# A new place for one product, four PSUM banks instead of six, and a rule for starting half-array steps

## The chip, the cores and the metric

One core of one Trainium2 chip runs the whole kernel. The metric is device time in microseconds (us), lower is better; it is the time of one execution, and of several executions the median counts. PE is TensorE (matrix products into PSUM, which has eight banks), DVE is VectorE, ACT is ScalarE, POOL is GpSimd, and SP issues the DMAs.

## The reference

Four batches of eight heads go through sliding-window attention with a few sink positions; the result is mixed along the sequence by a rank-32 product and sent through a two-layer network with a residual.

```
scores = scale * q @ k.T               # 768 positions, head size 64, 8 heads, 4 batches
keep = (pos_k < n_sink) | (0 <= pos_q - pos_k < window)
a = softmax(where(keep, scores, -1e9))
x = (a @ v), heads side by side        # (4, 768, 512)
h = x.transpose(0, 2, 1) @ U @ V       # rank 32, along the sequence
u = x + h.transpose(0, 2, 1)
out = u + maximum(u @ w_ch1, 0) @ w_ch2   # 512 -> 2048 -> 512
```

## The kernel before

The kernel doesn't issue instructions as it walks through the work. It first collects **steps** (class `Plan`): each is a short piece of work for one engine (some may run on one of two or three engines), with the tiles that it reads and writes, and a priority. `Plan.order` then runs a list scheduler, `forward`, several times, keeps the best order, and the steps are issued in it, so that each engine's instructions stand in a fixed order. In `forward`, whenever an engine is free, the steps that are ready stand in `can`, sorted by priority, and the first is picked. PSUM banks are a ring of eight (`self.bank`): a step that opens a bank (`takes`) is ready only when a bank is free, and a bank is given back when the last step on it is done.

The steps on PE are of two kinds. **Half-array steps** (`tiled=True`) use 64 of the array's 128 rows or columns, two products side by side: the attention scores (line L665, one step is a query block of a head pair, two products into two banks) and the attention values (L750). All others use the whole array. The planner adds `SWITCH` to a step's duration when it changes from one kind to the other, and once a half-array step has run, it prefers further half-array steps that are ready. It has no rule for when a run of them may begin.

The order of the large pieces is: attention of batch 0; the network of batch 0 (`ffn`, L958 to L960 and L980) with the attention of batch 1 between; then the networks of batches 1, 2 and 3 (`ffn_joint`, nearly all of it L1118), with the attention of batches 2 and 3 between the products of batch 1's network. At the end of each attention the last blocks are transposed (L715), the sink columns are transposed (L827, "sink transposes" below) and mixed in (L840), and the columns are transposed and mixed (L857, L880, L881, L921). While batch 1's network runs, weight sums for later rounds are made (`prepare`, tiles `spare`) and sent to DRAM (`ws<-spare`) by DVE, POOL and ACT.

`ffn_joint` computes both layers on 2x2 blocks with seven block products instead of eight. It runs in two rounds for a batch, six in all. In each round, the first layer `l1` makes for four pairs of hidden blocks the four blocks `h[0]` to `h[3]` (named `x11`, `x12`, `x21`, `x22` after); then `second` adds seven products into three pairs of banks, called `A`, `E` and `C`. One call of `second` runs over the four pairs and writes both banks of its pair: 4 x 2 x 3 matmuls of 128x384. `A` goes on accumulating over four calls, `E` over two, and `C` has one. After each call `gather` has DVE add both banks to result tiles (L1123), and a later call on the same bank may start only when that read is done. The calls before, in the order in which they are written:

```
A(x11) E(x12-x11) A(x22-x11) C(x21) A(x22-x12) E(x22) A(x21-x11)
```

As the bank pair `C` is opened while `A` and `E` are both in use, six banks are held at that point, and two are left for the attention steps and for the next round's first layer.

Of the kernel before, what the change touches and what calls it, by code (L numbers as in the profile page):

```python
# [42 lines left out]
ROUNDS = 14  # L43
SLACK = 0.0344
SWITCH = 0.2
BACKLOG = 3.0
SAME = 0.11
PRICE = {"DVE": 3.0, "ACT": 1.5, "POOL": 1.5}
# [218 lines left out]
class Plan:  # L267
# [91 lines left out]
    def forward(self):  # L359
# [9 lines left out]
        def at(s, e):  # L369
# [6 lines left out]
                return max(t, free[n - 1] if len(free) >= n else 1e12)  # L376
            return t

        def elsewhere(s, e, end):

            for x, (dur, _, _) in s.ways.items():
                if x != e:
                    t = max(avail[x], at(s, x))
                    queue = sum(o.ways[x][0] for o in ready[x]
                                if (o.prio, o.n) < (s.prio, s.n) and at(o, x) <= t and len(o.ways) == 1)
                    if t + queue + dur * PRICE[x] < end - 1e-9:
                        return True
            return False
# [8 lines left out]
        done = 0  # L397
        while done < len(self.steps):
            turn = sorted((max(avail[e], min(at(s, e) for s in lst)), e) for e, lst in ready.items() if lst)
            pick = None  # L400
            for t, e in turn:
                if t > 1e11:
                    break
                can = sorted((s for s in ready[e] if at(s, e) <= t + 1e-9), key=lambda s: (s.prio, s.n))
                if e == "PE" and tiled:
                    can.sort(key=lambda s: not s.tiled)
                pick = next((s for s in can if len(s.ways) == 1 or not elsewhere(s, e, t + s.ways[e][0] * PRICE[e])), None)
                if pick is not None:
                    break
            if pick is None:  # L410
                t, e = turn[0]
                pick = min((s for s in ready[e] if at(s, e) <= t + 1e-9), key=lambda s: (s.prio, s.n))
            s = pick
# [63 lines left out]
class Fast:  # L477
# [625 lines left out]
    def ffn_joint(self, b, prio):  # L1103
# [90 lines left out]
        def gather(banks, to, out=None):  # L1194
# [7 lines left out]
        wa = lambda layer, j, o: lambda i: (self.wd[layer][i], lambda: self.wd[layer][i]()[  # L1202
            :, :, CORNER[(j, o) if layer == 0 else (o, j)]])
        wc = lambda layer, k: lambda i: (self.ws[layer][i], lambda: self.ws[layer][i]()[:, :, k])
        x11, x12, x21, x22 = range(4)
        r11, r22, r12, r21 = (rest(o, c) for o, c in ((0, 0), (1, 1), (0, 1), (1, 0)))
        for start in range(0, NF // 2, ROUND):
            pairs = range(start, start + ROUND)
            last = pairs[-1] == NF // 2 - 1
            done = lambda o, c: (o, c) if last else None  # L1210
            for i in pairs:
                l1(i)
                prio += 7.3
            A, E, C = ([self.bank(), self.bank()] for _ in range(3))
            second(A, x11, wa(1, 0, 0), True)
            gather(A, r11)
            second(E, x11, wc(1, 0), True, (x12, x11))
            gather(E, r22)
            second(A, x11, wc(1, 1), False, (x22, x11))
            gather(A, r12)  # L1220
            second(C, x21, wa(1, 1, 0), True)
            gather(C, r11, done(0, 0))
            second(A, x12, wc(1, 2), False, (x22, x12))
            gather(A, r22, done(1, 1))
            second(E, x22, wc(1, 3), False)
# [392 lines left out]
```

## Time and profile before

| What | us |
|---|---|
| three timed runs | 699.42, 699.63, 703.04 |
| their median | 699.63 |
| the profiled execution | 701.17 |
| span of its instructions | 699.4 |
| PE busy | 677.2 (97% of the span) |
| DVE busy | 540.2 (77%) |
| ACT busy | 441.2 (63%) |
| POOL busy | 268.9 (38%) |

The profiled execution has 1.8 us outside its span of instructions. A busy PE may still run slower than it could: a matmul of 128x384 is shown with 0.33 to 0.34 us, since matmuls are pipelined, and what tells its cost is the time from one start to the next. The granted clock of PE is a share of its full speed.

### The profile page before, as it was taken

The page shows a single profiled execution, that of the slowest core. Times are in us where ns is not written, and L with a number is a line of the kernel's source. Part 1 is how long each engine was busy: PE and PEld are TensorE (multiplying, and loading weights), DVE is VectorE, ACT ScalarE, POOL GpSimd, SP SyncE. Part 2 cuts the span into 40 slices and gives each one's busy share as a digit, 9 for nine tenths or more (in the row PEclk, how much of TensorE's full clock was granted, in tenths as well). Part 3 has the DMA queues.
Part 4 walks back from the last instruction along what each step waited for, and adds up shares of the span by engine and source line. Part 5 has one row for each costly group of instructions (what it writes and reads, how often), then busy time and mean ns, then how long its engine had stood idle before and what let it go on. Part 6 is the DMA issues. An engine that isn't in the chain of part 4 may idle for free.

```text
span 699.4 us, 12892 instructions
## 1 busy us (share of the span) xinstructions
PE 677.2 (97%) x3986; PEld 598.0 (85%) x3986; DVE 540.2 (77%) x1493; ACT 441.2 (63%) x1192; POOL 268.9 (38%) x305
## 2 busy tenths in 40 slices
PE   7988799999999999999999999999999999999996
PEld 6666678787889978878878889989999998999996
DVE  7999989999986976868886999746747975673673
ACT  5988678759585477976776786345426634543551
POOL 3565575646373433735554574300200330020020
PEclk9999999999999999999999999999999999999999
DMA  8559797999976689885789764899888899888885
GB/s 276 169 176 355 246 375 264 351 310 396 370 249 230 248 271 355 274 270 182 241 291 322 263 225 128 287 363 292 252 249 253 251 294 354 256 250 249 254 253 192
DMA packets 135118, 190.37 MB, mean 272 GB/s; under 512 B 10240, under 2 KB 106112, under 8 KB 135040
## 3 DMA queue, kind: packets, MB, share of 16 engines
q1 hardware_dynamic: 134752, 189.06, 81.4%
q8 instruction: 34, 0.56, 0.3%
q10 hardware_dynamic: 288, 0.39, 0.2%
q14 instruction: 44, 0.36, 0.2%
HBM read 140.91 MB, written 48.50 MB: 271 GB/s over the span
## 4 chain that ended last, share of the span: by engine, by line
PE 76%; DVE 15%; DMA 4%; ACT 3%; issue 1%; POOL 0%; DVEq 0%; ACTq 0%; POOLq 0%
PE bank L1118 47%; PE bank L980 8%; PE bank L665 5%; PE bank L750 3%; PE bank L958 2%; PE bank L959 2%; PE bank L960 2%; PE bank L715 2%; DVE spare L548 2%; DMA ws<-spare 2%; DMA w<-wd 2%; DVE nt L132 1%; DVE p L674 1%; DVE w L548 1%; DVE bank L672 1%
## 5 line engine op out<-in xcount | busy, mean ns | idle before, releaser
L1118 PE MATMUL bank<-w,w 128*128 128x384 f32 x1044 | 206.6, 339 | 0.2 <-DMA w<-ws 0.2
L1118 PEld LDWEIGHTS bank<-w,w 128*128 128x128 f32 x1044 | 183.0, 189 | 4.2 <-DMA w<-ws 2.1
L550 POOL TENSOR_TENSOR w<-uh,w 128x384 fp32r<-128x384 f32 x18 | 19.7, 1092 | 165.9 <-ACT w L541 161.0
L677 ACT ACTIVATE p<-p,mn 128x132 f32<-128x132 f32 x192 | 75.9, 398 | 8.8 <-DVE mn L674 8.2
L1118 PE MATMUL bank<-spare,w 128*128 128x384 f32 x336 | 76.4, 342 | 0.7 <-ACT xhl L541 0.6
L133 POOL TENSOR_TENSOR spare<-nt,big 128x512 int32<-128x512 int32 x32 | 52.3, 1639 | 42.9 <-DVE nt L132 19.4
L980 PE MATMUL bank<-w,hh 128*128 128x512 f32 x192 | 63.5, 412 | 2.8 <-ACT w L541 2.4
L1123 DVE TENSOR_TENSOR big<-bank,big 128x384 f32<-128x384 f32 x84 | 44.6, 553 | 27.8 <-PE bank L1118 27.1
L1118 PEld LDWEIGHTS bank<-spare,w 128*128 128x128 f32 x336 | 59.1, 188 | 5.8 <-issue 3.7
L550 POOL TENSOR_TENSOR spare<-spare 128x128 f32<-128x128 f32 (+1 forms) x52 | 37.9, 739 | 56.2 <-DVE spare L548 16.1
L665 PE MATMUL bank<-kp,qp 64*128 64x260 f32 (+1 forms) x360 | 53.5, 406 | 0.0
L674 DVE CUSTOM_DVE_ANT_0 p<-bank,mask 128x132 f32<-128x132 f32 x192 | 50.3, 287 | 3.1 <-PE bank L665 2.3
L672 DVE COPY_PREDICATED bank<-past,bank 128x128 f32<-128x128 int32 x160 | 41.3, 289 | 7.4 <-PE bank L665 6.9
L958 PE MATMUL bank<-ul,w 128*128 128x384 f32 x128 | 45.1, 353 | 0.0
L980 PEld LDWEIGHTS bank<-w,hh 128*128 128x128 f32 x192 | 35.2, 192 | 11.6 <-ACT w L541 2.7
L665 PEld LDWEIGHTS bank<-kp,qp 64*128 64x128 f32 x360 | 31.7, 194 | 14.9 <-issue 5.9
L541 ACT COPY nt<-bank 128x384 f32<-128x384 f32 x35 | 16.6, 475 | 44.0 <-PE bank L1118 44.0
L548 DVE TENSOR_TENSOR spare<-spare 128x128 f32<-128x128 f32 (+1 forms) x98 | 39.2, 422 | 6.1 <-DMA ws<-spare 3.7
L725 POOL TENSOR_SCALAR_AFFINE_SELECT oph<-oph 128x384 f32<-128x384 f32 x64 | 36.0, 579 | 19.6 <-ACT oph L541 19.5
L959 PE MATMUL bank<-uh,w 128*128 128x384 f32 x128 | 43.2, 337 | 0.0
L960 PE MATMUL bank<-uh,w 128*128 128x384 f32 x128 | 43.2, 337 | 0.0
L750 PE MATMUL bank<-oph,vp 128*64 128x256 f32 (+1 forms) x448 | 42.9, 341 | 0.0
(245 smaller groups left out, 1588.4 us busy)
## 6 DMA issues: line engine op xcount, KB each, us to landing
w<-ws SPq DMA_DIRECT2D x192, 256.0 KB, 3.9
w<-wd SPq DMA_DIRECT2D x144, 256.0 KB, 4.1
big<-in_w_dram SPq DMA_DIRECT2D x32, 512.0 KB, 5.9
ws<-spare SPq DMA_DIRECT2D x32, 512.0 KB, 4.9
wd<-w SPq DMA_DIRECT2D x32, 384.0 KB, 5.8
kp<-in_k_dram SPq DMA_DIRECT2D x12, 396.0 KB, 4.8
qp<-in_q_dram SPq DMA_DIRECT2D x12, 384.0 KB, 5.4
vp<-in_v_dram SPq DMA_DIRECT2D x12, 384.0 KB, 4.3
```

The costliest lines, as they stand in the source:

```text
L133: {"POOL": lambda: nc.gpsimd.tensor_tensor(out() if out else x(), words(t())[:, :n], x(), ALU.add)},
L548: ways = {"DVE": (dve(n), lambda: nc.vector.tensor_tensor(dst(), a(), b(), op), pool)}
L550: ways["POOL"] = (gps(n), lambda: nc.gpsimd.tensor_tensor(dst(), a(), b(), op), True)
L665: nc.tensor.matmul(st()[:, :wd], qr()[at, q0:q0 + P], kr()[at, k0:k0 + wd], start=True, stop=True)
L674: add("DVE", dve(SW), lambda st=st, row=row, at=at, wd=wd, qb=qb, mn=mn: nc.vector.tensor_tensor_reduce(row(), st()[:, wd - SW:wd], self.m ...
L677: add("ACT", act(SW) + 0.22, lambda row=row, at=at, mn=mn, sm=sm: nc.scalar.activation(row(), row(), AF.Exp, bias=at(mn), scale=-1.0, accu ...
L750: nc.tensor.matmul(pa()[i * D:(i + 1) * D, at:at + hi - lo], vr()[:, i, kb, :], mv, start=first, stop=last, skip_group_check=True)
L958: nc.tensor.matmul(ph()[:, :CH], wh, ul()[:, c, :], start=n == 0, stop=False)
L959: nc.tensor.matmul(ph()[:, :CH], wl, uh()[:, c, :], start=False, stop=False)
L960: nc.tensor.matmul(ph()[:, :CH], wh, uh()[:, c, :], start=False, stop=n == NC - 1)
L980: nc.tensor.matmul(acc[k](), a()[:, sl], w()[:, :, at, m:m + P].rearrange("p d o j -> p o d j"), start=not begin and i == 0 and j == 0, st ...
L1118: nc.tensor.matmul(bank()[:, :CH], w()[:, at:at + P], u()[:, d, :] if n > 1 else u(), start=first and i == 1, stop=last and i == 3 * n, sk ...
```

## The change

Two edits that do not depend on each other. In `forward`, when PE last ran a whole-array step and both kinds are ready, half-array steps are taken out of `can` unless at least `TOGETHER` = 2 of them are ready and the ring has banks for two, or one has been ready for more than `HOLD` = 3.0 us; if nothing else is ready, they stay. In `ffn_joint`, the product into `C` is written first instead of fourth, and its `gather` comes before that of `A`; the first output block is sent out after `A`'s sum instead of `C`'s. `C`'s banks are given back before `E` is opened, so four banks are held at a time, not six. The new order of the calls, in which two calls on `A` now follow each other:

```
C(x21) A(x11) E(x12-x11) A(x22-x11) A(x22-x12) E(x22) A(x21-x11)
```

```diff
@@ -43,6 +43,8 @@
 SLACK = 0.0344
 SWITCH = 0.2
+TOGETHER = 2
+HOLD = 3.0
 BACKLOG = 3.0
@@ -376,6 +378,9 @@
                 return max(t, free[n - 1] if len(free) >= n else 1e12)
             return t
 
+        def free(s, t):
+            return sum(f[0] <= t for f in s.takes[0].ring.free) if s.takes else 0
+
@@ -404,6 +409,11 @@
                 can = sorted((s for s in ready[e] if at(s, e) <= t + 1e-9), key=lambda s: (s.prio, s.n))
                 if e == "PE" and tiled:
                     can.sort(key=lambda s: not s.tiled)
+                elif e == "PE":
+                    few = [s for s in can if s.tiled]
+                    if few and len(few) < len(can) and (
+                            len(few) < TOGETHER or sum(len(s.takes) for s in few[:TOGETHER]) > free(few[0], t)):
+                        can = [s for s in can if not s.tiled or t - at(s, e) > HOLD] or can
@@ -1212,14 +1222,14 @@
             A, E, C = ([self.bank(), self.bank()] for _ in range(3))
+            second(C, x21, wa(1, 1, 0), True)
+            gather(C, r11)
             second(A, x11, wa(1, 0, 0), True)
-            gather(A, r11)
+            gather(A, r11, done(0, 0))
             second(E, x11, wc(1, 0), True, (x12, x11))
             gather(E, r22)
             second(A, x11, wc(1, 1), False, (x22, x11))
             gather(A, r12)
-            second(C, x21, wa(1, 1, 0), True)
-            gather(C, r11, done(0, 0))
             second(A, x12, wc(1, 2), False, (x22, x12))
             gather(A, r22, done(1, 1))
             second(E, x22, wc(1, 3), False)
```

The steps are the same ones in number and kind, but the whole program is ordered anew, after the first 28 rows of PE. Lines behind the edits are numbered up to 10 higher in the changed kernel (L665 is L675 there, L1118 is L1128). Counted over the whole order, PE changes into half-array steps and back 61 times before and 49 times after: 9 and 9 times in batch 0's attention, 19 and 15 in batch 0's network, 33 and 25 in batch 1's network. Runs of a single score step number 20 before and 2 after.

**First place, PE,** at the start of batch 3's attention, in batch 1's network. Before (`kp`, `qp` are keys and queries, L880 and L881 the mixing of batch 2):

```order
L1118 MATMUL bank2_163<-w4_173,w3_172 128x384 x2
L665 MATMUL bank3_164<-kp0_462,qp0_471 128x132
L665 MATMUL bank0_161<-kp0_462,qp0_471 128x132
L1118 MATMUL bank6_167<-w5_174,w3_172 128x384
L1118 MATMUL bank6_167<-w4_173,w3_172 128x384 x2
L1118 MATMUL bank2_163<-w5_174,w3_172 128x384 x3
L665 MATMUL bank4_165<-kp0_462,qp0_471 128x260
L665 MATMUL bank3_164<-kp0_462,qp0_471 128x260
L1118 MATMUL bank6_167<-w5_174,w3_172 128x384 x3
L880 MATMUL bank5_166<-xhl0_2501,ust0_681 128x512
L881 MATMUL bank5_166<-xhl1_2513,ust0_681 128x512
L665 MATMUL bank0_161<-kp0_462,qp0_471 128x260
```

The same place after:

```order
L675 MATMUL bank5_166<-kp0_468,qp0_478 128x132
L675 MATMUL bank0_161<-kp0_468,qp0_478 128x132
L675 MATMUL bank7_168<-kp0_468,qp0_478 128x260
L675 MATMUL bank1_162<-kp0_468,qp0_478 128x260
L1128 MATMUL bank2_163<-w5_174,w3_172 128x384 x3
L1128 MATMUL bank6_167<-w5_174,w3_172 128x384 x3
L890 MATMUL bank3_164<-xhl0_2604,ust0_447 128x512
L891 MATMUL bank3_164<-xhl1_2610,ust0_447 128x512
L1128 MATMUL bank2_163<-w5_174,w3_172 128x384 x3
L675 MATMUL bank5_166<-kp0_468,qp0_478 128x260
L675 MATMUL bank0_161<-kp0_468,qp0_478 128x260
L675 MATMUL bank4_165<-kp0_468,qp0_478 128x260
```

The first five score steps of the head pair stand in five runs of one before, and in a run of two and a run of three after (its last rows are not shown).

**Second place, DVE,** at the end of batch 2's attention. The reciprocal (L687, L697 after) of the last softmax sums is waited for by the last transposes on PE; the rows on `spare` belong to `prepare` and may wait for a `ws<-spare` DMA. Before:

```order
L687 RECIPROCAL r_3590<-r_3590 128x6
L674 ISA p1_2911,mn_3588<-bank0_161,mask_97 128x132
L674 ISA mn_3588 128x1
L542 CAST hh0_3047<-ul1_3507 128x384
L548 TENSOR_TENSOR spare1_176<-spare1_176 128x128
L548 TENSOR_TENSOR hh1_3051<-ul1_3507,hh0_3047 128x384
L548 TENSOR_TENSOR spare1_176<-spare1_176 128x128
L542 CAST hl0_3152<-uh0_3018 128x384
L548 TENSOR_TENSOR ul1_3507<-ul1_3507 128x384
L687 RECIPROCAL r_3645<-r_3645 128x6
```

After:

```order
L684 ISA p1_2943,mn_3603<-bank7_168,mask_97 128x132
L684 ISA mn_3603 128x1
L731 TENSOR_TENSOR oph0_3679<-bank4_165,tri_113 128x2x128
L731 TENSOR_TENSOR oph1_3685<-bank1_162,tri_113 128x2x128
L1133 TENSOR_TENSOR big0_89<-bank0_161,big0_89 128x384
L697 RECIPROCAL r_3697<-r_3697 128x6
L558 TENSOR_TENSOR spare1_176<-spare1_176 128x128
L552 CAST w5_174<-uh0_2979 128x384
```

Before, six instructions, two of them on `spare`, stand between the last score block's minimum and the reciprocal; after, three stand there, none of them on `spare`, and the row on `spare` follows the reciprocal.

**Third place, PE,** in the last round of batch 3's network, around the third call on `A`. Before (`A` is bank2 and bank5, `C` is bank6 and bank1):

```order
L1118 MATMUL bank6_167<-hh1_3051,w2_171 128x384
L1118 MATMUL bank6_167<-hh0_3047,w2_171 128x384 x2
L1118 MATMUL bank1_162<-hh1_3051,w2_171 128x384
L1118 MATMUL bank1_162<-hh0_3047,w2_171 128x384 x2
L1118 MATMUL bank6_167<-hl1_3160,w2_171 128x384
L1118 MATMUL bank6_167<-hl0_3152,w2_171 128x384 x2
L1118 MATMUL bank1_162<-hl1_3160,w2_171 128x384
L1118 MATMUL bank1_162<-hl0_3152,w2_171 128x384 x2
L1118 MATMUL bank2_163<-w4_173,w3_172 128x384 x3
L1118 MATMUL bank5_166<-w4_173,w3_172 128x384 x3
```

After (`A` is bank0 and bank5, `E` ends in bank1):

```order
L1128 MATMUL bank0_161<-hl1_3241,w2_171 128x384
L1128 MATMUL bank0_161<-hl0_3227,w2_171 128x384 x2
L1128 MATMUL bank5_166<-hh1_3149,w2_171 128x384
L1128 MATMUL bank5_166<-hh0_3130,w2_171 128x384 x2
L1128 MATMUL bank5_166<-hl1_3241,w2_171 128x384
L1128 MATMUL bank5_166<-hl0_3227,w2_171 128x384 x2
L1128 MATMUL bank1_162<-w5_174,w3_172 128x384
L1128 MATMUL bank1_162<-w4_173,w3_172 128x384 x2
L1128 MATMUL bank0_161<-w4_173,w3_172 128x384 x3
L1128 MATMUL bank5_166<-w4_173,w3_172 128x384 x3
```

Before, all 24 matmuls of `C` stand between `A`'s second and third call. After, 9 matmuls stand between bank0's last product and its next one (6 of bank5, 3 of bank1), and 6 for bank5.

## Rows read from the trace of the kernel before

**Rows 1.** The page's first section: busy time, share and instructions of each engine.
```profile
PE 677.2 (97%) x3986; PEld 598.0 (85%) x3986; DVE 540.2 (77%) x1493; ACT 441.2 (63%) x1192; POOL 268.9 (38%) x305
```

**Rows 2.** Stretches: length; PE, PEld, DVE, ACT, POOL busy; granted clock; DMA share, GB/s.
```profile
0.00:100.00 100.00, 87.28 (x494) 67.11 (x496) 88.28 (x307) 76.24 (x226) 54.64 (x68) 0.97 0.76 259
100.00:240.00 140.00, 139.93 (x802) 115.84 (x799) 126.50 (x339) 100.25 (x269) 79.53 (x80) 1.00 0.86 308
240.00:448.00 208.00, 205.64 (x1314) 175.16 (x1313) 172.45 (x552) 154.02 (x474) 106.31 (x135) 0.99 0.78 255
448.00:700.00 252.00, 244.34 (x1382) 239.87 (x1380) 153.01 (x297) 110.69 (x225) 28.46 (x23) 1.00 0.85 271
```

**Rows 3.** Timeline of PE: start us, us, instruction, count; whole-array products alone.
```profile
520.10 1.21 PE L1118 MATMUL bank<-spare,w 128*128 128x384 f32 x6
521.15 1.20 PE L1118 MATMUL bank<-w,w 128*128 128x384 f32 x6
```

**Rows 4.** Timeline of PE: a run of three score steps and a single one.
```profile
381.99 1.58 PE L665 MATMUL bank<-kp,qp 64*128 64x260 f32 x12
383.51 1.34 PE L1118 MATMUL bank<-w,w 128*128 128x384 f32 x6
384.78 0.71 PE L665 MATMUL bank<-kp,qp 64*128 64x260 f32 x4
385.42 0.44 PE L1118 MATMUL bank<-spare,w 128*128 128x384 f32 x1
```

**Rows 5.** Timeline of PE: the end of batch 2's attention; in brackets idle time and releaser.
```profile
311.75 0.49 PE L715 MATMUL bank<-ident,p 128*128 128x128 f32 x3
311.99 0.77 PE L1118 MATMUL bank<-w,w 128*128 128x384 f32 x3
313.35 0.92 PE L715 MATMUL bank<-ident,p 128*128 128x128 f32 x3 [0.60 <-ACT p L695]
314.48 0.55 PE L715 MATMUL bank<-ident,p 128*128 128x128 f32 x3 [0.20 <-POOL p L698]
314.78 0.77 PE L1118 MATMUL bank<-w,w 128*128 128x384 f32 x3
315.86 0.71 PE L827 MATMUL bank<-ident,first0q 128*128 128x128 f32 x3 [0.31 <-ACT first0q L541]
316.22 2.27 PE L1118 MATMUL bank<-w,w 128*128 128x384 f32 x6
318.29 0.84 PE L827 MATMUL bank<-ident,first0k 128*128 128x128 f32 x3
318.79 1.47 PE L1118 MATMUL bank<-hh,w 128*128 128x384 f32 x5
```

**Rows 6.** The stretch of low clock within it, columns as in Rows 2.
```profile
316.08:319.49 3.41, 3.41 (x14) 3.31 (x13) 2.50 (x5) 2.65 (x8) 1.85 (x3) 0.51 0.58 181
```

**Rows 7.** Timelines of DVE and ACT ahead of these transposes.
```profile
310.35 0.29 DVE L548 TENSOR_TENSOR spare<-spare 128x128 f32<-128x128 f32 x1 [1.46 <-DMA ws<-spare]
...
312.68 0.18 DVE L687 RECIPROCAL r<-r 128x6 f32<-128x6 f32 x1
...
312.89 0.99 ACT L695 ACTIVATE p<-p,r 128x132 f32<-128x132 f32 x3 [2.00 <-DVE r L687]
...
313.58 0.85 POOL L698 TENSOR_TENSOR p<-p,r 128x396 f32<-128x396 f32 x1
```

**Rows 8.** Timeline of PE: the end of batch 3's attention.
```profile
414.31 0.69 PE L1118 MATMUL bank<-w,w 128*128 128x384 f32 x3
415.65 0.97 PE L840 MATMUL bank<-pst,vsh 128*128 128x384 f32 x4 [0.65 <-DVE pst L548]
...
425.88 0.40 PE L880 MATMUL bank<-xhl,ust 128*128 128x512 f32 x1
426.78 0.50 PE L881 MATMUL bank<-xhl,ust 128*128 128x512 f32 x1 [0.50 <-DVE xhl L548]
```

**Rows 9.** The page's groups: the sums that read the banks after each call.
```profile
L1123 DVE TENSOR_TENSOR big<-bank,big 128x384 f32<-128x384 f32 x84 | 44.6, 553 | 27.8 <-PE bank L1118 27.1
```

## The prediction, as it was put on record

> **What bounds the kernel now.** I read the page's engine totals first [rows 1]: PE is busy 97% of the span of 699.4 us, the next engine, DVE, 77%. Then a table of stretches, to see where this holds [rows 2]. In the first 100 us, batch 0's attention and the first weights, PE is idle for 13 us while DVE is at 88%: there the chain through DVE sets the pace. From 100 us on PE is busy nearly always, in batch 0's network (100 to 240), in batch 1's (240 to 448) and in the last two (448 to 700). So a change counts in these stretches if it takes time out of PE's own stream, and busy time doesn't show that; the distance from one start to the next does. Whole-array products of 128x384 start every (521.15 - 520.10) / 6 = 0.175 us [rows 3]. What PE needs beyond that is what the change can give back or add. The timeline of PE shows two places where it does: each run of half-array steps, and the ends of the attentions, where the steps depend on each other.
>
> **The change, part by part.**
>
> *Fewer runs of half-array steps.* Four stretches follow each other [rows 4]: a run of three score steps takes 383.51 - 381.99 = 1.52 us (12 matmuls of the trace are three steps), six whole-array products 1.27, a run of one step 0.64. Two steps more cost 0.88 us, 0.44 each, so 0.64 holds 0.20 us that belong to the run. The six products took 1.27 instead of 6 x 0.175 = 1.05, so 0.22 us more are lost where they take over and give back. One run costs 0.20 + 0.22 = 0.42 us beside its steps; I take 0.40, since the 0.175 is the tightest spacing there is and mixed products have slightly more. [...]
>
> The order holds 61 runs before and 49 after, 4 fewer in batch 0's network and 8 fewer in batch 1's, both bound by PE: 12 x 0.40 = 4.8 us less. The lower bound is 8 x 0.40 = 3.2: in batch 0's network DVE is busy 126.5 of 140 us [rows 2], so 1.6 us won on PE there could be lost waiting for DVE.
>
> *Longer runs.* They need banks while they go on: each step opens two, and what frees them is a copy and a reduction on DVE. With four instead of six banks held by the second layer, two steps fit at once; a third waits for DVE. Bounds: 0 where banks are free, as in the run of three above, and 0.3 us a run for some 10 runs of three or more. I take +0.5 us.
>
> *The end of batch 2's attention.* This is the worst place after the first 100 us. From 311.99 to 318.79 PE runs 12 whole-array products and four transposes of three blocks [rows 5]. At 0.175 and at 0.24 (311.99 - 311.75) that is 2.10 + 0.96 = 3.06 us; it took 6.80, so 3.74 were lost. Half of it is idle or slow around the transposes, which wait for the scaled weights `p`. [...] What was late? ACT waited 2.00 us for the reciprocal, which DVE ran at 312.68; ahead of it on DVE stands a `spare` row that sat 1.46 us until a `ws<-spare` DMA had landed [rows 7]. The two transposes that wait for it lost 313.35 - 311.99 - 0.52 = 0.84 and 314.48 - 313.35 - 0.24 = 0.89 us, together less than these 2.00. In the new order the `spare` rows stand behind this reciprocal, so the 2.00 us go. But its cover on PE shrinks: between the last score step and the first of these transposes the order had 30 whole-array products and has 24 now, 6 x 0.175 = 1.05 us less. The first transpose, 0.84 late before, would be 0.84 - 2.00 + 1.05 = -0.11: just in time. [...] I take 3.2 of the 3.74 us as gained; bounds 0 (something else is late) and 3.74.
>
> *The other ends.* At the end of batch 3's attention PE waited twice: 415.65 - 414.31 = 1.34 us for three products (0.8 lost) because the sink mixing needs `pst`, which ACT and DVE make from the sink transposes; and 0.90 us for one product of the column mixing that needs `xhl` (0.67 lost, against 0.23 us without a wait) [rows 8]. In the new order batch 3 has 12 instead of 9 products to cover the first wait and 9 instead of 6 for the second, so most of both goes. But batches 1 and 2 now have what batch 3 had: all 24 column transposes in one piece with only 6 short products ahead of the mixing, and in batch 2 9 products between the sink transposes and their mixing. By the same rows that is 2 x 0.67 + 0.8 = 2.1 us new, about 1.1 gone: +1.0 us, bounds -1.1 and +2.1.
>
> *`A` after `A`.* A call on `A` may start when DVE has read the bank. A read takes 0.55 us [rows 9], the two banks' reads follow each other on DVE, and the rows of the third place leave 9 products (1.6 us) for the first bank and 6 (1.05) for the second. Before, 24 products (4.2 us) stood there. DVE has 39% idle after 448 us [rows 2], and with a signal each way the second read just fits if DVE is free. What is queued behind a late read on DVE is the making of the next call's operands. Six rounds have one such turn each: 0 where the cover holds, 1.0 us (both reads, uncovered) where it is gone, so 0 to 6 us. I take 0.7.
>
> *At no cost:* `C` first. Its operand `x21` is the last that the first layer makes, but only the fourth pair needs that; the three pairs before it are 18 products, 3.2 us, over a ReLU, a cast and a subtraction of about half a us each. If that cover went, it would be some 2 us a round. Its four weight DMAs a round move ahead of `A`'s on SP, none is added, and the DMA load after 448 us (0.85) stays. The first 100 us have nine runs before and after, and the work ahead of the first network is the same to within a few rows on DVE: 0, with 1.5 us either way for a new order.
>
> **The sum:** -4.8 + 0.5 - 3.2 + 1.0 + 0.7 = -5.8 us. Against the profiled span of 699.4 that is 693.6, or 695.4 for the profiled execution (701.17, 1.8 us outside the span). The median of the shown runs is 1.5 us below that execution, so I set the gain against the median: 699.63 - 5.8 = **693.8 us**. For this kernel some 0.5%, 3.5 us, is what a measurement can tell from no change.
>
> **The rivals.**
>
> *The time comes out elsewhere (no change).* The runs are fewer, but the new order has its own late chain. For it: such a stall is made by chance of order, as the `spare` row was, and sixteen of these sums with their DMAs still lie in batch 1's network. Against it: there is one such stall of over 1 us on PE in 340 us before. Price: with the 3.7 us of [rows 5] at another place and the ends at +2.1, -4.8 + 0.5 + 2.1 + 0.7 = -1.5: 698.1 us.
>
> *DVE takes back what PE wins.* Batch 0's network is at 90% on DVE, the start at 88% [rows 2]. Then the 1.6 us there are lost and the start is 1.5 us longer: 696.9 us, also within the bound.
>
> *Four banks starve PE (slower).* At each `A`-`A` turn DVE comes late, PE stops for 1.0 us, and its clock falls as in [rows 6]: half speed for 3.4 us costs 1.7. Six turns are 16 us, instead of the 0.7 above: 709 us. It decides from about 10 us lost at the turns in all (6.5 won elsewhere and 3.5 beyond), that is four of six turns with a fallen clock. Against it: after 448 us the clock is 1.00 throughout with banks read between products all the time [rows 2]. [...]
>
> **How the numbers follow.** Forecast as summed, 690.5 to 696.0: 0.62. Stall elsewhere: 0.19. DVE takes it back: 0.13. Starved: 0.06. That the change doesn't do what it says is no case, since the order holds the 49 runs. The first case is faster by more than 0.5% (below 696.1), the middle two lie within, with 0.02 of theirs beyond on the slow side, where several stalls meet. Faster 0.62, same 0.30, slower 0.08. The likeliest case alone has 690.5 to 696.0; the range goes on to 699.5, over most of the middle two cases, and leaves out about 2 in 10.
>
> **What would show it.** Half-array runs in PE's timeline: 49, each still with 0.4 us beside its steps. Granted clock 1.00 from 100 us to the end, and no wait of the last transposes of batch 2 over 0.3 us. The sink mixing or `xhl` waits now in batches 1 and 2. Waits of PE for the sums of L1133 at six places, under 0.3 us each. It would be wrong if the clock falls anywhere after 100 us, if a DVE row on `spare` waits ahead of softmax work, or if the first network begins more than 2 us later.

## The result, and the profile after

The change made the kernel slower: a median of 704.99 us (nine runs, 703.19 to 707.82) against 699.94 us for the kernel before (nine runs, 698.60 to 703.48), a ratio of 1.0068 with a 95% interval of 1.0043 to 1.0093. The profiled execution took 704.28 us, with a span of 702.6 us instead of 699.4.

The page's engine totals and one group, which answer to [rows 1, 9] (the lines of `kernel.py` are up to ten higher now):

```profile
PE 673.0 (96%) x3986; PEld 598.2 (85%) x3986; DVE 536.4 (76%) x1506; ACT 435.5 (62%) x1197; POOL 266.0 (38%) x305
...
L1133 DVE TENSOR_TENSOR big<-bank,big 128x384 f32<-128x384 f32 x84 | 44.5, 552 | 26.1 <-PE bank L1128 26.1
```

PE is busy for 4.2 us less, yet the span is 3.2 us longer, so PE stands idle more. The stretches of [rows 2], now, say where:

```profile
0.00:100.00 100.00, 85.40 (x471) 65.01 (x472) 87.69 (x298) 75.32 (x227) 49.70 (x67) 0.91 0.74 253
100.00:240.00 140.00, 137.85 (x800) 114.07 (x799) 117.82 (x339) 95.00 (x268) 69.20 (x72) 1.00 0.84 305
240.00:448.00 208.00, 206.72 (x1344) 180.02 (x1343) 181.51 (x582) 150.99 (x470) 114.37 (x137) 1.00 0.81 266
448.00:700.00 252.00, 243.07 (x1376) 239.07 (x1374) 149.36 (x290) 114.18 (x233) 32.70 (x31) 1.00 0.84 266
```

By 100 us PE has run 471 matmuls, 23 fewer than before, at a mean granted clock of 0.91 instead of 0.97. From 240 to 448 us it has run 30 more, and the clock is 1.00.

To compare kernels by stage I work out **lost time**: from each matmul's start to the next, less the spacing that its shape has in an undisturbed row (0.174 us for 128x384, 0.231 for 128x512, and so on), summed. The rest, 619 us, is the same work in all kernels. I take three stages: the *start* (to the first product of batch 1's network, 245.9 us before and 251.4 after), the *middle* (to the last product of the last attention, 445.4 and 454.3), and the *tail*. Lost time of the profiled executions, in us:

```
            start   middle  tail    sum
before      43.1    25.4    5.6     74.1
changed     47.9    19.6    9.5     77.0
difference  +4.8    -5.8    +3.9    +2.9
```

**The middle went as forecast.** This is PE's timeline at the end of batch 2's attention in the changed kernel, which answers to [rows 5]:

```profile
319.98 0.49 PE L725 MATMUL bank<-ident,p 128*128 128x128 f32 x3
320.23 1.30 PE L1128 MATMUL bank<-hl,w 128*128 128x384 f32 x6
321.36 0.49 PE L725 MATMUL bank<-ident,p 128*128 128x128 f32 x3
321.61 0.77 PE L1128 MATMUL bank<-w,w 128*128 128x384 f32 x3
322.22 0.49 PE L837 MATMUL bank<-ident,first0q 128*128 128x128 f32 x3
322.55 0.49 PE L837 MATMUL bank<-ident,first0k 128*128 128x128 f32 x3
322.79 1.83 PE L1128 MATMUL bank<-w,w 128*128 128x384 f32 x9
325.42 0.79 PE L850 MATMUL bank<-pst,vsh 128*128 128x384 f32 x3 [0.79 <-DVE pst L558]
```

No transpose waits, six products take 321.36 - 320.23 = 1.13 us, and the clock does not fall (1.00 from 240 to 448 us, as above). The new wait is for `pst`, 0.79 us, where the prediction put 0.8; PE shows none of the `xhl` waits that it put at 0.67 each at the ends of batches 1 and 2.

**The start.** The longest waits of PE in the first 100 us of the changed kernel (us in total, times, longest):

```profile
PE bank L931 <- DVE t L918: 3.6, 1, 3.6
PE bank L990 <- ACT w L551: 3.3, 1, 3.3
PE bank L990 <- DVE w L558: 1.6, 1, 1.6
```

In the kernel before, the longest waits at these two lines were 2.6, 2.4 and 0.9 us. This is PE's timeline at the second and third of them:

```profile
80.88 0.34 PE L970 MATMUL bank<-uh,w 128*128 128x384 f32 x1
84.52 0.80 PE L990 MATMUL bank<-w,hh 128*128 128x512 f32 x1 [3.30 <-ACT w L551]
86.94 0.80 PE L990 MATMUL bank<-w,hh 128*128 128x512 f32 x1 [1.62 <-DVE w L558]
```

And these are the windows of low clock in the start (columns as in [rows 2]):

```profile
15.80:22.60 6.80, 6.49 (x28) 4.38 (x29) 5.47 (x38) 4.86 (x20) 3.04 (x5) 0.50 0.43 141
63.60:67.00 3.40, 3.40 (x12) 3.40 (x12) 3.37 (x8) 3.40 (x9) 2.91 (x3) 0.50 1.00 325
84.10:90.90 6.80, 4.76 (x10) 3.43 (x11) 6.30 (x14) 2.60 (x5) 2.66 (x2) 0.50 0.75 276
```

The granted clock is 0.50 behind the first wait and from the end of the second on, and once earlier, 17.0 us in all; before it was 6.8 us, at 60 and 84 us.

Of the 4.8 us, 2.1 are lost before the first network begins (66.7 us instead of 64.6) and 2.7 in batch 0's network. There PE also waits for DVE after 100 us (100 to 251.4 us), where the kernel before shows no wait:

```profile
PE bank L990 <- DVE hl L979: 1.5, 2, 1.4
PE bank L968 <- DVE hl L979: 0.5, 1, 0.5
```

**The tail.** PE's timeline in the last round of the changed kernel, at the turn from one call on `A` to the next:

```profile
680.79 0.69 PE L1128 MATMUL bank<-hh,w 128*128 128x384 f32 x3
681.32 0.69 PE L1128 MATMUL bank<-hl,w 128*128 128x384 f32 x3
681.85 0.69 PE L1128 MATMUL bank<-hh,w 128*128 128x384 f32 x3
682.38 0.70 PE L1128 MATMUL bank<-hl,w 128*128 128x384 f32 x3
682.91 4.85 PE L1128 MATMUL bank<-w,w 128*128 128x384 f32 x27
688.45 1.31 PE L1128 MATMUL bank<-w,w 128*128 128x384 f32 x6 [0.69 <-DMA w<-ws]
```

The chain that ended last, in order of time (start us, us, what), over the same place:

```profile
677.83 5.78 PE bank L1128 x33
683.61 0.13 SPq L566
...
683.84 4.57 DMA w<-ws
688.40 0.04 issue
688.45 4.65 PE bank L1128 x25
```

Here PE doesn't wait for a bank. It waits for a weight piece, whose DMA could not be issued until PE had freed the piece's slot at 683.61; it took 4.57 us to land. The planner hides the bank's read: it takes the last products of the first of the two `A` calls bank by bank (the blocks of three above) and puts a product of `E` behind them, so PE comes through the last pieces in another order and the slots come free in a bunch. By the starts, the turns cost 0.48 + 1.32 us at 563.8 and 567.4 and 0.85 at 687.4, for weight pieces. At the turn between, the blocks are six and six, and there PE does wait for the bank, as the prediction had it. PE's timeline, and DVE's with the two reads:

```profile
623.34 1.22 PE L1128 MATMUL bank<-hl,w 128*128 128x384 f32 x6
624.68 5.48 PE L1128 MATMUL bank<-w,w 128*128 128x384 f32 x30
624.07 1.09 DVE L1133 TENSOR_TENSOR big<-bank,big 128x384 f32<-128x384 f32 x2 [0.49 <-PE bank L1128]
```

From start to start PE takes 1.34 us instead of 1.05, so this turn costs 0.29 us, and the turns 2.9 in all. The kernel before has no such waits there. One more stall of 1.3 us, at 468.6 us, is for DVE's sum into `uh`, which reads a bank of the first layer (the bank is the only tile that it shares with the products behind it), and one of 1.5, at 474.2, is for a weight piece. PE's waits from 455 to 480 us:

```profile
PE bank L1128 <- DMA w<-wd: 1.5, 2, 1.3
PE bank L1128 <- DVE uh L1133: 1.1, 1, 1.1
```

### The profile page after: what moved, and what is told of

The parts are those of the page before. It is cut to its first block, busy times and chain, and to the rows that moved or that the text cites. A ratio compares the mean times of both kernels' runs of the same rounds, so it can differ in the third digit from the quotient of the medians.

```text
span 702.6 us, 12908 instructions
## 1 busy us (share of the span) xinstructions
PE 673.0 (96%) x3986; PEld 598.2 (85%) x3986; DVE 536.4 (76%) x1506; ACT 435.5 (62%) x1197; POOL 266.0 (38%) x305
## 4 chain that ended last, share of the span: by engine, by line
PE 72%; DVE 12%; DMA 8%; ACT 4%; issue 1%; POOL 1%; SPq 0%; ACTq 0%; DVEq 0%; POOLq 0%
PE bank L1128 46%; PE bank L990 6%; PE bank L675 5%; PE bank L760 4%; DMA w<-ws 2%; PE bank L725 2%; PE bank L968 2%; DMA w<-wd 2%; DVE spare L558 2%; PE bank L969 2%; PE bank L970 2%; DVE w L558 2%; DMA qp<-xd 2%; ACT p L687 1%; DVE nt L134 1%
## 5 line engine op out<-in xcount | busy, mean ns | idle before, releaser
L1128 PE MATMUL bank<-w,w 128*128 128x384 f32 x1044 | 205.5, 338 | 2.6 <-DMA w<-ws 2.2
L1128 PEld LDWEIGHTS bank<-w,w 128*128 128x128 f32 x1044 | 182.2, 188 | 8.0 <-DMA w<-ws 2.5
L687 ACT ACTIVATE p<-p,mn 128x132 f32<-128x132 f32 x192 | 75.9, 397 | 18.6 <-DVE mn L684 18.6
L1128 PE MATMUL bank<-spare,w 128*128 128x384 f32 x336 | 74.9, 339 | 1.6 <-DVE uh L1133 1.1
L135 POOL TENSOR_TENSOR spare<-nt,big 128x512 int32<-128x512 int32 x32 | 48.4, 1516 | 43.3 <-DVE nt L134 25.3
L560 POOL TENSOR_TENSOR uh<-uh 128x384 f32<-128x384 f32 x16 | 17.5, 1094 | 121.6 <-DVE w L558 67.2
L1128 PEld LDWEIGHTS bank<-spare,w 128*128 128x128 f32 x336 | 59.4, 188 | 3.6 <-DVE uh L1133 1.4
L675 PE MATMUL bank<-kp,qp 64*128 64x260 f32 (+1 forms) x360 | 51.3, 397 | 0.6 <-DVE mn L684 0.6
L560 POOL TENSOR_TENSOR spare<-spare 128x128 f32<-128x128 f32 (+1 forms) x46 | 33.0, 731 | 46.9 <-ACT spare L551 32.9
L735 POOL TENSOR_SCALAR_AFFINE_SELECT oph<-oph 128x384 f32<-128x384 f32 x64 | 34.4, 555 | 33.7 <-ACT oph L551 30.5
L558 DVE TENSOR_TENSOR spare<-spare 128x128 f32<-128x128 f32 (+1 forms) x104 | 43.6, 449 | 4.2 <-DMA ws<-spare 2.7
L675 PEld LDWEIGHTS bank<-kp,qp 64*128 64x128 f32 x360 | 31.8, 190 | 13.8 <-issue 4.2
L760 PEld LDWEIGHTS bank<-oph,vp 128*64 128x64 f32 x448 | 29.9, 139 | 15.9 <-issue 4.4
L970 PE MATMUL bank<-uh,w 128*128 128x384 f32 x128 | 43.2, 337 | 0.0
```

Source lines behind the costliest of these rows:

```text
L135: {"POOL": lambda: nc.gpsimd.tensor_tensor(out() if out else x(), words(t())[:, :n], x(), ALU.add)},
L558: ways = {"DVE": (dve(n), lambda: nc.vector.tensor_tensor(dst(), a(), b(), op), pool)}
L560: ways["POOL"] = (gps(n), lambda: nc.gpsimd.tensor_tensor(dst(), a(), b(), op), True)
L675: nc.tensor.matmul(st()[:, :wd], qr()[at, q0:q0 + P], kr()[at, k0:k0 + wd], start=True, stop=True)
L687: add("ACT", act(SW) + 0.22, lambda row=row, at=at, mn=mn, sm=sm: nc.scalar.activation(row(), row(), AF.Exp, bias=at(mn), scale=-1.0, accu ...
L760: nc.tensor.matmul(pa()[i * D:(i + 1) * D, at:at + hi - lo], vr()[:, i, kb, :], mv, start=first, stop=last, skip_group_check=True)
```

## The experiments

Three theories. **Draw:** the planner makes a new order for the whole kernel out of any edit, each order has its own late transfers, and that of before loses little. **Rule:** what the rule on half-array runs does to the order costs or gives time by itself. **Products:** the new sequence of products costs time by itself, at the turns. The times of before, run beside each, had medians of 701.54 (e1 to e4), 700.11 (e5 to e8), 700.03 (e9 to e12), 700.74 (e13 to e15) and 700.58 us (e16 to e18). Ratios and intervals are to these.

### One edit at a time, and none (e1 to e4)

e1 is the changed kernel with the old sequence of products, e2 the kernel before with the new one and no rule. e3 and e4 are the kernel before and the changed kernel with one constant of the planner moved by 5%, which no edit depends on:

```diff
-SWITCH = 0.2
+SWITCH = 0.21
```

> The changed kernel with the product into C back in fourth place (six banks), so only the rule for half-array runs is new; the order has 49 such runs. Seen so far, the changed kernel wins 6 us in batch 1's network and loses 2 in batch 0's attention, 3 in batch 0's network and 4 after all attention is done. Theory 'draw' (each reordering of the program draws its own late transfers and waits, whatever the edit; only the fewer runs are a sure gain of some 4 us): no edit owns the losses, so this kernel is 2 to 5 us faster than before where its draw is a mean one, and its losses in the first 250 us and in the last 250 us differ from the changed kernel's by 2 us or more each. Theory 'rule' (holding score steps back makes the first attention and the first network later): the first 250 us lose 4 to 5 us as in the changed kernel, the last 250 us are as before, in all 699 to 700. Theory 'products' (four banks and the new sequence of products make the last networks wait): the loss after the attentions is gone, in all 700 to 701 with the same loss at the start, or 696 if the start too came from the products.

> The kernel before with only the new sequence of products (C first, four banks), no rule for half-array runs; the order has 59 such runs instead of 61. Theory 'draw': anywhere from 697 to 705, with losses at places that are not those of the changed kernel. Theory 'products': the stretch after the attentions loses some 4 us as in the changed kernel, at the same six places, and the first 250 us are as before: 703 to 704. Theory 'rule': 698 to 700, nothing lost in the last 250 us or the first 250.

> The kernel before with one planner constant moved by a hair (SWITCH 0.2 to 0.21): neither edit, the same steps, but another order (59 runs of half-array steps instead of 61, 12 of a single step instead of 20). Theory 'draw': the order alone moves the time by 2 us or more, more likely up than down, since the order of before was a good draw: 699 to 705, and the losses in the first 250 us and after the attentions differ from before by 1 to 3 us each. Theories 'rule' and 'products': within 1.5 us of before, 698.5 to 701.5.

> The changed kernel with SWITCH 0.21 instead of 0.2: both edits, another order (47 half-array runs instead of 49). Theory 'draw': differs from the changed kernel's 705 by 2 us or more, more likely down: 697 to 703, and the long waits at 58, 81, 84, 124, 469, 474 and 567 us are not all there again. Theories 'rule' and 'products': the same losses again, 703.5 to 706.5.

Medians, ratios with intervals, and lost time:

```
                    us      ratio   interval        start  middle tail
e1 rule alone       708.42  1.0104  1.0078-1.0130   51.8   25.4   4.6
e2 products alone   710.85  1.0149  1.0122-1.0177   49.1   24.6   8.2
e3 before, redrawn  707.18  1.0085  1.0060-1.0110   47.7   26.8   6.3
e4 changed, redrawn 705.62  1.0068  1.0041-1.0096   48.5   23.3   5.9
```

e1, e2 and e3 are slower than any theory had them (at most 701, 705 and 705 us), and e4 lies where Rule and Products put it (703.5 to 706.5), above Draw's 697 to 703. A 5% change of one constant costs the kernel before 0.85%, more than the change itself. So a comparison of whole kernels says little about either edit: the draw decides at least as much.

### The start kept (e5 to e8)

To take the draw of the start away, the planner first makes the order of before, then keeps each step that it starts ahead of batch 1's network on its engine and at its planned time; only later steps are planned anew, with or without the edits:

```diff
-            t = s.ready[e]
+            t = max(s.ready[e], self.cut if s.pin is None else s.pin + 1e6 - 1e-9)
...
+        old = Fast(*self.args)
+        cut = PIN(old, old.layout())
+        self.first_product, self.plan.rule, self.plan.switch = FIRST, RULE, SWITCHES[1]
+        self.pins, self.plan.cut = {s.key: (s.start, s.eng) for s in old.plan.steps if s.start < cut}, cut
```

> The kernel before, with neither edit: every engine's order is kept word for word up to batch 1's network (the first 925 rows of TensorE, 643 of VectorE, 199 of SyncE), and only what follows is planned anew (27 half-array runs there for 33). The theory 'draw' (an order drawn anew loses to late transfers wherever it is new; the order of before happened to lose little in its first 250 us) expects the loss of the first 250 us at 43 us, as before, where the five reordered kernels have 47.7 to 51.8, and the rest within 2 us of 31: 699 to 704 us. Its rival (the chip's own scatter, not the order, made the start of the five long) expects a start of 47 or more here too.

> As e5 with the same kept start, and the rule on the half-array runs behind it (24 runs, 1 of a single step). 'Rule pays' expects the stretch of batch 1's network and the attention under it 2 to 6 us under e5's, the tail as e5's: 695 to 699 us, below the kernel before. 'Rule is a draw too' expects the stretch within 1.5 us of e5's: 699 to 704.

> As e5 with the same kept start, and the new sequence of the products behind it, without the rule (28 runs). 'Products cost' expects 2 to 4 us more loss than e5 in the joint network of the last batches, with TensorE waiting 0.8 us or more for weight pieces of ws where A's third product follows A's second: 702 to 707. 'Products are free' expects no such waits and e5's time within 1.5 us.

> As e5 with the same kept start, and both edits behind it (23 runs): the change without its new start. If the start was what the change lost (2.1 and 2.7 us to batch 1's network), 'draw' expects 698 to 702 us, so no longer slower than before: the rule's 2 to 6 us less in the attention, the products' 2 to 4 us more in the tail. If the change loses by what it does, it is still 704 to 707.

```
                    us      ratio   interval        start  middle tail
e5 neither edit     705.24  1.0087  1.0059-1.0115   41.8   26.1   9.4
e6 rule             697.40  0.9960  0.9938-0.9981   43.2   23.3   4.6
e7 products         703.79  1.0054  1.0032-1.0076   42.1   23.1   11.3
e8 both             703.04  1.0064  1.0040-1.0087   41.6   23.3   8.5
```

The start loses 41.6 to 43.2 us in all four, as before: with the order kept, its loss is kept. But e5 missed its time. It lost 9.4 us in the tail without the new sequence; one line of its PE timeline explains 3.4 of them, a wait for a weight piece in an order without either edit:

```profile
460.59 0.41 PE L1142 MATMUL bank<-p,w 128*128 128x384 f32 x1 [3.42 <-DMA w<-wd]
```

Behind it the granted clock is 0.50 from 461.8 to 465.2 us, and the 12 products there lose another 1.6 us. So the draw is at work behind the start as well. e6 beats both kernels, and its tail has no wait at the places of the turns.

e7 lies in its range, 702 to 707 us, but 1.5 us below e5, not above it. Its costliest turn has blocks of six and six, so slots in a bunch aren't the only way to such a wait, and the clock falls behind it (PE's timeline, and a window with columns as in [rows 2]):

```profile
563.07 3.37 PE L1142 MATMUL bank<-w,w 128*128 128x384 f32 x11 [3.09 <-DMA w<-ws]
563.60:567.00 3.40, 3.40 (x13) 3.40 (x12) 1.65 (x5) 0.92 (x2) 0.00 (x0) 0.51 0.41 141
```

That fall costs 1.6 us more. e8 has the same wait, 2.84 us, without a fall.

The rule's gain depends on what stands beside it. With the old products it is 7.8 us (e5 to e6), of which e5's wait and clock are some 5, and 2.7 against the kernel before, which has the same start; with the new ones it is 0.7 us (e7 to e8), within the noise, and the middle is the same, 23.1 and 23.3.

e8 is 5.6 us above e6, 3.9 of them in the tail. It missed its forecast of 698 to 702 by 1 us in the median; its profiled execution, 700.27 us, was the shortest of ten (700.27 to 706.96), so the stage sums of single executions carry some 2 to 3 us of scatter beside the medians.

### The sequence of products alone, in the last four rounds (e9 to e12)

Here the order is kept up to the second layer of batch 2's first round, where the attentions are over and the rule has nothing to do. e9 plans the rest anew with the new sequence (practically the changed kernel), e10 with the old one; e11 is e6 with the new sequence from there on. e12 is a redrawn e6 (SWITCH at 0.21 behind the kept start).

```diff
+            first = (b, start) in self.rounds
+            for at in ("CAEF" if first else "AEFC"):
```

`F` stands for the second call on `A`, and `self.rounds` lists the rounds with the new sequence: all six in e9, the first two in e10, the last four in e11.

> The changed kernel with its order kept up to the second layer of the last four rounds (the first 1634 rows of TensorE) and the rest planned anew with the same sequence of products: 21 of 3063 rows of TensorE differ from the changed kernel's. Every theory expects the changed kernel's time, 703 to 707 us, and its waits for pieces of ws where A's product follows A's, 2.5 to 4.2 us in the last three rounds. It is the base for e10, on the same chip.

> As e9, with the old sequence of products in the last four rounds alone: all before them is word for word the changed kernel's. 'Products cost' expects the waits of the changed kernel at its three A-after-A turns (1.8, 0.3 and 0.9 us at 563.8 to 567.4, 624.2 and 687.4) gone, and 2 to 4 us less than e9: 700 to 704. 'Products are free, those waits are drawn with the order' expects as many waits at other places and e9's time within 1.5 us.

> The reverse of e10: the kernel of e6 (old start, rule, old sequence, 697.4 us) with the new sequence of products in its last four rounds alone. 'Products cost' expects waits for ws of 2 to 4 us at the A-after-A turns near 558, 622 and 685 us, which e6 does not have, and 2 to 4 us more than e6: 699 to 702. 'Products are free' expects e6's time within 1.5 us: 696 to 699.

> The kernel of e6 (old start, rule behind it, old sequence of products) with the planner's price of a switch at 0.21 behind the start, which draws another order from row 987 of TensorE on (23 runs for 24). If the rule itself made e6 fast, 695 to 700 us; if e6 was only a good draw of that order, 701 to 706, as the reorderings without the rule.

```
                      us      ratio   interval        start  middle tail
e9 changed            706.37  1.0074  1.0047-1.0100   49.5   22.0   9.2
e10 changed, old tail 702.99  1.0041  1.0023-1.0059   48.8   20.5   6.2
e11 e6, new tail      702.92  1.0029  1.0014-1.0044   43.5   22.8   10.5
e12 e6 redrawn        697.66  0.9966  0.9947-0.9986   41.7   24.6   5.5
```

Undoing the sequence takes 3.4 us off the median and 3.0 off the tail (2.8 off the mean, give or take 2); doing it to e6 adds 5.5 us (697.40 to 702.92) and 5.9 in the tail, more than the 2 to 4 expected. This is the last round of e10 by PE's timeline: six and six instead of three and three, and no wait.

```profile
680.86 1.22 PE L1142 MATMUL bank<-hh,w 128*128 128x384 f32 x6
681.92 1.22 PE L1142 MATMUL bank<-hl,w 128*128 128x384 f32 x6
682.98 5.37 PE L1142 MATMUL bank<-w,w 128*128 128x384 f32 x30
```

And of e11, where the pattern of the changed kernel is back:

```profile
682.32 0.69 PE L1142 MATMUL bank<-hl,w 128*128 128x384 f32 x3
682.85 4.85 PE L1142 MATMUL bank<-w,w 128*128 128x384 f32 x27
688.31 1.31 PE L1142 MATMUL bank<-w,w 128*128 128x384 f32 x6 [0.61 <-DMA w<-ws]
```

But not all of e11's cost is weights. At another of its turns DVE is busy with rows queued ahead of the banks' reads until 502.28 us, and PE waits for the read:

```profile
502.88 2.37 PE L1142 MATMUL bank<-w,w 128*128 128x384 f32 x12 [1.18 <-DVE big L1147]
```

"Products cost" holds. e12, another draw behind the same start, has e6's time, so e6 was hardly a single lucky order; two draws are few.

### Is the longer start a draw? (e13 to e18)

Three more redrawn kernels without the edits (the planner's slack at 0.036 and 0.040 instead of 0.0344 us; its first backlog at 3.5 us instead of 3.0), then the changed kernel with the same three constants.

```diff
-SLACK = 0.0344
+SLACK = 0.036
```

> The kernel before with the planner's slack at 0.036 for 0.0344 us: neither edit, another order from the first rows on. If the order of before was a good draw, the loss of the first 250 us is 46 to 52 us, as in e3 (47.7), not 43, and the time 703 to 710. If the two edits lengthened the start, it is 42 to 45 and the time 699 to 703.

> As e13, with the slack at 0.040. The same two expectations: a start of 46 to 52 us lost and 703 to 710 us if before was a good draw, 42 to 45 and 699 to 703 if the edits lengthened the start.

> As e13, with the planner's idea of the queue's first backlog at 3.5 us for 3.0. The same two expectations: a start of 46 to 52 us lost and 703 to 710 us if before was a good draw, 42 to 45 and 699 to 703 if the edits lengthened the start.

> Both edits with the planner's constant of e13 (slack 0.036 for 0.0344 us), its partner without the edits: 699.05 us, 41.3 us lost before batch 1's network. If a start is a draw and nothing else, this one's is anywhere from 41 to 52 us, on the mean of the three pairs within 2 us of 45.6; if the edits lengthen the start, all three are at 48 or above. Behind the start the rule gives 2 and the products cost 3, so the time stands 1 us above e13's plus the difference of the starts.

> Both edits with the constant of e14 (slack 0.040), its partner without the edits: 701.8 us, 44.9 us lost in the start. The same two expectations as e16: a start from 41 to 52 us, or at 48 and above; the time 1 us above e14's plus the difference of the starts.

> Both edits with the constant of e15 (first backlog 3.5 us), its partner without the edits: 707.77 us, 50.7 us lost in the start. The same two expectations as e16: a start from 41 to 52 us, or at 48 and above; the time 1 us above e15's plus the difference of the starts.

```
                    us      ratio   interval        start  middle tail
e13 no edit         699.05  0.9967  0.9938-0.9997   41.3   24.3   6.1
e14 no edit         701.80  1.0023  0.9999-1.0048   44.9   24.7   5.6
e15 no edit         707.77  1.0104  1.0050-1.0158   50.8   24.4   6.1
e16 both edits      706.19  1.0081  1.0059-1.0104   48.8   19.3   8.6
e17 both edits      706.16  1.0081  1.0054-1.0108   46.4   23.4   6.1
e18 both edits      706.51  1.0103  1.0048-1.0158   46.2   26.3   7.2
```

Both plain expectations failed for e13 to e15: they spread over the whole range, 41.3 to 50.8 us, with times from 699 to 708. e16 to e18 fit a plain draw (their mean is 47.1, within 2 us of 45.6); not all are at 48 or above, so "the edits lengthen the start" isn't shown for the start as a whole. e16 came out as almost the changed kernel's order (in the traces, 34 of PE's 3986 matmuls stand otherwise), so it is a repeat, not a new draw. The differences of the pairs' times were +7.1, +4.4 and -1.3 us; 1 us plus the difference of the starts would be +8.5, +2.5 and -3.6. The five different orders without edits lose 45.6 us on average in the start, the four with both (changed, e4, e17, e18) 47.3. That difference, some 2 us, lies within the spread.

The traces do show a part of it. Ahead of the first network, where PE runs 344 matmuls before and after, the orders fall apart by the rule. The first network begins at 64.7 to 68.6 us, 67 on average, in the eight kernels ordered with the rule from the beginning (changed, e1, e4, e9, e10, e16 to e18), and at 61.6 to 64.8, 63 on average, in the twelve others. e1, the rule alone, has 67.8; e2, the products alone, 61.6. So with the rule batch 0's attention takes some 4 us longer; this grouping was read from the traces afterwards, and by what chain the rule does it was not followed. In batch 0's network the draw is wider: the orders without edits differ there by some 8 us.

## Why the prediction was wrong

**The step that failed first: "the first 100 us ... 0, with 1.5 us either way for a new order".** The same few rows on DVE don't make the same start. The start lost 4.8 us more. Of these, 2.1 us came before the first network, where the prediction had 0: over all orders the rule delays the first network by some 4 us, and the kernel before is one of the later ones without it. The other 2.7 came in batch 0's network, where the four runs fewer were forecast at -1.6 and at worst 0; that lies well within the draw there. Five orders without any edit show the size that the start's term has: 41.3 to 50.8 us, so some 5 us either way, not 1.5. With the start kept (e5 to e8) the loss stayed at 41.6 to 43.2. The kernel before has a good start but not the only one, since e13's is shorter. I named this sign ("the first network begins more than 2 us later"; it began 66.7 - 64.6 = 2.1 us later, the second 5.5) and gave it no case of its own.

**The step that failed second: "`A` after `A`: +0.7".** It measured about +3.0 (e9 against e10) to +5.9 (e6 against e11). The place was right, and the mechanism that I named was the smaller part. I asked whether DVE reads the bank in time, and that wait is there, at 0.29 us in the changed kernel's last three rounds, where I expected under 0.3 a turn, and once each at 1.36 us in e2 and 1.18 in e11, more than the 1.0 I set as its bound. I didn't ask which other ring the same products pass through: the weight pieces, which cost 2.65 of the 2.94 us at these turns. In all ten kernels with the new sequence in the last rounds PE stands at these turns, by 2.1 to 4.2 us in the last three rounds, and in none of the ten others at 620 to 628 or 684 to 692 us. (The 2.1 to 4.2 are not weights alone: each has the 0.3 us for a bank, and e2 and e18 wait for DVE's operands at the first of the three.) On average their tails lose 8.5 against 6.0 us. That the sequence costs this is shown by e10 and e11; that it goes through slots that come free in a bunch is read from the chain above for one turn, e7 and e8 show a long wait without it, and no run gave the pieces more slots.

**Right in the changed kernel's own trace.** The 49 runs are there, and batch 2's end lost its stall and its fall of the clock. The -3.2 us for that end took the low clock of [rows 6] (0.51) to go with the idle time; no run shows that the one follows from the other, and e8 waits 2.84 us without a fall. What the changed kernel shows is nine products and four transposes from 319.98 to 322.79 us in 2.81 us, some 0.3 more than 9 x 0.175 + 4 x 0.24 = 2.54, at a granted clock of 1.00. The middle's terms sum to -3.2 (eight runs) + 0.5 - 3.2 + 1.0 = -4.9 us; it measured -5.8. A run still has a price beside its steps. PE's timeline of the changed kernel with runs of two, between products of six:

```profile
276.69 1.15 PE L675 MATMUL bank<-kp,qp 64*128 64x260 f32 x8
277.77 1.32 PE L1128 MATMUL bank<-w,w 128*128 128x384 f32 x6
278.94 1.20 PE L1128 MATMUL bank<-spare,w 128*128 128x384 f32 x6
```

That is (1.08 - 0.88) + (1.17 - 1.05) = 0.32 us, for the 0.40 taken. But as a gain of the rule, 5.8 us is partly this draw's: over all kernels the middle loses 22.8 us on average with the rule (twelve profiles, 19.3 to 26.3) and 24.9 without (eight, 23.1 to 26.8). Counted once for each order (changed, e9, e10 and e16 have one there, e6 and e11 another), it is 23.7 with the rule, so the rule's share is some 1 to 2 us, less than either spread. The stall of [rows 5] is an accident of before's order, since no other of the twenty traces has a fall of the clock in the middle; the rule did not have to undo it. Behind a kept start and with the old products, kernels with the rule took 697.4 and 697.7 us, 2.5 below before and 7.7 below e5.

**The rivals.** "The time comes out elsewhere" named the right cause, a new order with its own late chain, but gave it 3.7 us at one place; it was 4.8 in the start, beside the tail. "Four banks starve PE" was wrong for the changed kernel: its clock is 1.00 from 100 us nearly to the end, with all its waits for weights, and its waits for banks in the tail are the 0.29 us at a turn and 1.1 us in the first layer. Only e7 had a fall at a turn, behind one wait of 3.09 us for a weight piece. "DVE takes back what PE wins" was nearer than its chance of 0.13: PE waits 2.0 us for `hl` of DVE in batch 0's network, as shown above, and the start is longer. That DVE is less busy from 100 to 240 us, 117.8 instead of 126.5, doesn't keep a single row of it from being late.

**What stays open:** by what chain the rule delays the first network, what the edits do in batch 0's network, whether more slots would free the turns, and why executions of one order scatter by up to 6.7 us (e8).

## What to carry to other kernels

Where a planner orders the whole kernel, first redraw the unchanged kernel a few times with a constant that shouldn't matter: here that alone gave 699 to 708 us, and an edit worth 3 us can't be judged until the order around it is kept, stage by stage. When products change places, follow every ring that they pass through, the weight slots as well as the PSUM banks, and ask in what order slots come free and how long the transfer that waits for them takes. Judged in this way the two edits fall apart. Behind batch 0's network, and with the old products, the rule goes with the two fastest kernels that keep the start of before (697.4 and 697.7 us); ahead of it the rule costs, and beside the new products it gains nothing that can be measured. The new sequence isn't worth keeping.

## What was unexpected of the hardware

Transfers issued close together landed later in this stretch. In the changed kernel's last round the pieces of `ws` (256 KB each) issued at 680.98, 682.57, 683.18 and 683.84 us landed after 3.5, 3.5, 4.0 and 4.6 us, and those of `wd` behind them, spaced by 1.0 us, after 4.4, 4.1 and 3.7. The last piece of `ws` is the one that PE waits for. The view of the tile `w` from 680 to 690 us gives the ends of it:

```profile
L566 SPq DMA_DIRECT2D w<-ws x5: 518/518/562, 679.9 to 683.8; - x5
...
DMA to landing us min/median/max: 3.5/3.7/4.6
```

The granted clock of a start isn't fixed by the order: the changed kernel, e9 and e10 have the same order there, and 17.0, 27.2 and 10.2 us of low clock. The lost time hardly follows (47.9, 49.5 and 48.8 us), so in the start much of the low clock seems to fall where PE would wait anyway; there it mustn't be booked as a cost by its length. In the tail, where PE has work, 3.4 us of low clock cost 1.6 us in e5 and in e7.
